# A later, shorter stretch for the second layer's weight conversion, with its first loads one pair ahead

## The chip, the cores and the metric

One core of a Trainium2 chip runs the whole kernel. The metric is device time in microseconds (us) of one execution; the kernel before was timed three times. The engines are named as the profile names them: PE (TensorE matmuls), PEld (its weight loads), DVE (VectorE), ACT (ScalarE), POOL (GpSimd) and SP (the queue that issues every DMA here). Each engine works through its own list of instructions strictly in the order in which it was written.

## The reference

Retention attention over 8 batches, 8 heads, 576 positions, then two feed-forward layers over the 4608 tokens:

```python
ret = scale * (q @ k.T) * Dmat          # Dmat[i, j] = gamma**(i - j), lower triangle
x = ret @ v                             # reshaped to 4608 x 512
h = x @ w_in;  x = (h - tanh(h)) @ w_out                    # first layer, d_ff = 2048
h = x @ w_in2; out = (h * sigmoid(1.702 * h)) @ w_out2      # second layer
```

The feed-forward weights arrive as float64, as pairs of 32-bit words.

## The kernel before

Tokens go in 9 tiles of 512 (`NTILE`), the hidden dimension in 8 pairs of two 128-wide columns. The main loop runs over 72 steps, one for each pair p of each tile t of layer 1; below, "pair (3,0)" is the first pair of the fourth tile. Every float32 operand is held as a high and a low float16 part and multiplied in three products. One step computes two `h` blocks on PE (`mm_in`, L534, 24 matmuls, two PSUM buffers `h`), the activation on ACT and DVE (`act1`), and, two steps behind (`LAG`), the second product into four `y` banks (`mm_out`, L650, 24 matmuls). `act1` on DVE is, for a pair, two `z` (L551, each of which ends the use of one `h` buffer), two passes over `w` (L554, L555), a predicated copy (L556) and `gl` (L558). When a tile is through, ACT evicts `y` (L657).

Into these steps other work is dealt out. `prep_steps` prepares the next tile: its input `yf` is loaded from DRAM into the one buffer that there is, its maximum taken (L446 on DVE, a reduction over partitions on POOL, L115), the scale `sx` worked out in small DVE instructions (L106 to L111), and the parts `xh` (ACT, L491) and `xl` (DVE, L496) written. `bg` holds the attention chunks that are left, five thirds of chunks a step. After `bg` the second layer's weights are converted by `conversion_steps(2, ...)`: 16 units of 1 MB each are loaded (`f`, two buffers), ACT takes magnitudes (L175), DVE clamps, shifts and joins the words (L180, L183, L190, L192) and finds a maximum per block; then each block is scaled, combined into seven sums for a Strassen-like product (`wsum`, L224 to L227) and split into `wsh` (ACT, L240) and `wsl` (DVE, L241), which SP writes to DRAM (`pd`, `od`). When the conversion is through, `load_pair` and `load_out` load these weights (`ws`, `woh`, `wol`; L672, L677) for layer 2 (PE L577, L625).

The program is recorded in the order of these loops, but a scheduler then orders each engine's instructions anew, with its own estimate of durations, before the kernel runs. So the order on the engines is not the order of the loops; it is fixed once the program is built. Attention, recorded by step 15, stands on PE up to pair (2,7). The pacing of the conversion is these lines of the main loop:

```python
elif conv2 is None:
    ...
    rate2 = len(conv2) / (n1 - LAST2 - i)
if conv2:
    todo_c += rate2
```

Of the kernel before, what the change touches and what calls it, by code (L numbers as in the profile page):

```python
# [47 lines left out]

LAG = 2
FIRST = 14  # L50
LAST2 = 10
NIP = 4
NF0 = 4
URGE = 600
# [20 lines left out]
def retention_two_ffn(ctx: ExitStack, tc: tile.TileContext, w1i, w1o, w2i, w2o, qt, kt, k, v, dq_d,  # L75
# [4 lines left out]
    def pool(name, bufs, space=None, to=ctx, side="left"):  # L80
        kw = {} if space is None else {"space": space}
        with tc.using_default_side(side):
            return to.enter_context(tc.tile_pool(name=name, bufs=bufs, reuse_waits="tile", **kw))
# [197 lines left out]
    def conversion_steps(l, kinds, w_in, w_out, fp, nf, wb, ahead, wp, also=None):  # L281
        units, load, magnitude, clamp, join, reduce, scale, split, bound, combine, split_seven = conversion(l, kinds, w_in, w_out, fp, wb, wp)
        blocks = [(kind, b) for kind in kinds for b in range(4)]
        steps = []

        def start():
            if also:
                also()
            for i in range(nf):
                load(i)  # L290
            magnitude(0)

        steps.append(start)
        for n, (kind, b) in enumerate(blocks):
            prev = blocks[n - 1] if n else None
            for u in range(2):
                i = 2 * n + u

                def one(i=i, u=u):
                    if not ahead and u == 0 and i:  # L300
                        magnitude(i)
                    clamp(i)
                    if ahead or u == 0:
                        magnitude(i + 1)

                def two(i=i):
                    join(i)
                    load(i + nf)

                steps += [one, two]  # L310
                if ahead and prev:
                    if u == 0:
                        steps.append(lambda p=prev: scale(*p))
                    steps.append(lambda p=prev, u=u: split(*p, u))
            steps.append(lambda kind=kind, b=b: reduce(kind, b))
            if (kind, b) == ("i", 3):
                steps.append(bound)
            if not ahead or n == len(blocks) - 1:
                steps.append(lambda kind=kind, b=b: scale(kind, b))
                if l == 2:  # L320
                    for q in range(2):
                        steps.append(lambda kind=kind, b=b, q=q: combine(kind, b, q))
                        steps.append(lambda kind=kind, b=b, q=q: split_seven(kind, b, q))
                else:
                    steps += [lambda kind=kind, b=b, u=u: split(kind, b, u) for u in range(2)]
        return deque(steps)
# [198 lines left out]
    def mm_in(l, t, c, hp_):  # L525
        o, j = L[l], jobs[l, t]
        blk, cc = divmod(c, 4)
        h = hp_.tile([P, TT], F32, tag="h", name="h")
        cs = slice(cc * P, (cc + 1) * P)
        n = 0  # L530
        for kd in range(KD):
            wh, wl = o.wih[blk][:, kd, cs], o.wil[blk][:, kd, cs]
            for w, x in ((wh, j.xh), (wh, j.xl), (wl, j.xh)):
                PE.matmul(h, w, x[:, kd, :], start=n == 0, stop=n == 3 * KD - 1)  # L534
                n += 1
        return h
# [4 lines left out]
    def act1(t, c, hs):  # L541

        j = jobs[1, t]
        blk = c // 4
        isig, sg = j.isig[:, blk : blk + 1], j.sg[:, 0:1]
        u, w, th, d, mk = wide("u"), wide("w"), wide("t"), wide("z"), wide("m", U8)
        gh, gl = wide("gh", F16, gp[-1]), wide("gl", BF16, gp[-1])
        for x, h in enumerate(hs):
            A.activation(out=u[:, x], in_=h, func=AF.Square, scale=isig)  # L549
            A.activation(out=th[:, x], in_=h, func=AF.Tanh, scale=isig)  # L550
            V.scalar_tensor_tensor(out=d[:, x], in0=h, scalar=isig, in1=th[:, x], op0=ALU.mult, op1=ALU.subtract)  # L551
        A.activation(out=w, in_=u, func=AF.Square, scale=SQ, bias=sqb)
        A.activation(out=mk, in_=th, func=AF.Square, scale=MASK_SCALE)
        V.scalar_tensor_tensor(out=w, in0=w, scalar=LEVEL, in1=u, op0=ALU.add, op1=ALU.mult)  # L554
        V.tensor_tensor(out=w, in0=w, in1=th, op=ALU.mult)  # L555
        V.copy_predicated(w, mk, d)  # L556
        A.activation(out=gh, in_=w, func=AF.Copy, scale=sg)  # L557
        V.scalar_tensor_tensor(out=gl, in0=w, scalar=sg, in1=gh, op0=ALU.mult, op1=ALU.subtract)  # L558
        newest[0] = d[:, 1, :1]
        for x in range(2):  # L560
            gtile[1, t, c + x] = gh[:, x], gl[:, x]
# [44 lines left out]
    def pair(t, p):  # L606
        act2(t, p, mm_pair(t, p))
# [61 lines left out]
    def load_pair(p):  # L669
        for parts, (sp, tag), src in zip((L[2].wih, L[2].wil), pair_slots(p), pair_d[p]):  # L670
            parts[p] = sp.tile([P, 7, 2, P], F16, tag=tag, name=f"ws{p}")
            SP.dma_start(parts[p], src)  # L672

    def load_out():
        for x, nm in enumerate(("woh", "wol")):
            w = wp2[0].tile([P, KF, DM], F16, tag=nm, name=nm + "2")
            SP.dma_start(w, out_d[x])  # L677
            setattr(L[2], nm, w)
# [9 lines left out]
    if True:  # L688
# [66 lines left out]
        conv2, cmb, loaded = None, [], False  # L755
        pre = deque()
        steps = [(t, p) for t in range(NTILE) for p in range(KF // 2)]
        n1 = len(steps)
        todo_c = 0.0
        for i in range(n1 + LAG):  # L760
            if i < n1:
                t, p = steps[i]
                act1(t, 2 * p, [mm_in(1, t, 2 * p + x, ps_h) for x in range(2)])
                if p == 1:
                    nl, nt = (1, t + 1) if t + 1 < NTILE else (2, 0)
                    items, scale_y = prep_steps(nl, nt)
                    pre.extend(items)
                    jobs[nl, nt].scale_y = scale_y
                for _ in range(2 if len(pre) > KF // 2 - p else 1):
                    if pre:  # L770
                        pre.popleft()()
                if bg:
                    for _ in range(min(5, len(bg))):
                        bg.popleft()()
                elif conv2 is None:
                    psa_scope.close()
                    att_scope.close()
                    ps_p.append(pool("ps_p", 2, PSUM))
                    fp = pool("fp2", 2, to=conv_scope, side="right")
                    wb = pool("wb2", 2, to=conv_scope, side="right")  # L780
                    cmb.append(pool("cmb", 1, to=conv_scope, side="right"))
                    stg = pool("stg", 2, to=conv_scope, side="right")
                    conv2 = conversion_steps(2, "io", w2i, w2o, fp, 2, wb, False, stg)
                    rate2 = len(conv2) / (n1 - LAST2 - i)
                if conv2:
                    todo_c += rate2
                    while conv2 and todo_c >= 1:
                        conv2.popleft()()
                        todo_c -= 1
                if conv2 is not None and not conv2 and not loaded:  # L790
                    loaded = True
                    conv_scope.close()
                    wp2.append(pool("wp2", 1))
                    for n in range(4):
                        load_pair(n)
                    load_out()
                    assert i < n1 - 8
                if t == NTILE - 1 and p in (5, 7):
                    load_pair(4 + p // 6)
            else:  # L800
                pair(0, i - n1)
            if i >= LAG:
                t, p = steps[i - LAG]
                for x in range(2):
                    mm_out(1, t, 2 * p + x)
# [58 lines left out]
```

## Time and profile before

| what | value |
|---|---|
| median of 3 runs | 1722.0 us (1721.31 to 1723.73) |
| the profiled execution | 1721.1 us |
| its span, first to last instruction | 1719.3 us |
| mean granted PE clock | 0.971 of full speed |
| PE busy | 1657.3 us, 96% |
| DVE busy | 1185.2 us, 69% |
| ACT busy | 847.3 us, 49% |

The profiled execution lies 0.9 us under the median; 1.8 us of it lie outside the span. Layer 1 runs from about 140 us to 1000 us, layer 2 from there to the end.

### The profile page before, as it was taken

What the parts mean: (1) busy time and instruction counts of PE and PEld (TensorE: products, weight loads), DVE (VectorE), ACT (ScalarE), POOL (GpSimd) and SP (SyncE); (2) the same over time, 40 slices, a digit from 0 to 9 for tenths busy, and PEclk for the clock granted to TensorE, in tenths of its full rate; (3) what the DMA queues carried; (4) which work ended last, traced back from release to release, by engine and by line L of the source; (5) the groups of instructions that cost most, each with busy time, mean ns of one, the idle gap of its engine ahead of it and who ended that gap; (6) DMA issues with size and microseconds to landing.
All of it is one profiled execution on the core that took longest, in us unless ns stands there. A gap on an engine that the chain in (4) does not pass through costs nothing.

```text
span 1719.3 us, 25499 instructions
## 1 busy us (share of the span) xinstructions
PE 1657.3 (96%) x10512; PEld 952.7 (55%) x10512; DVE 1185.2 (69%) x1982; ACT 847.3 (49%) x1263; POOL 31.5 (2%) x40
## 2 busy tenths in 40 slices
PE   5788999999979999999999999999999999999999
PEld 4664555555533444444444456666666666666665
DVE  7998665555589997998896864646556464646453
ACT  5556556556457676766666643333333232423222
POOL 0000000000000100000000000000000000000000
PEclk8668999999989999999999999999999999999999
DMA  9873324323053330432160120101011010100000
GB/s 336 277 247 118 107 86 120 99 74 115 22 196 113 116 106 11 123 104 76 37 236 25 68 93 1 50 1 50 1 50 44 7 50 1 50 1 25 1 25 25
DMA packets 111796, 141.36 MB, mean 82 GB/s; under 512 B 39488, under 2 KB 71360, under 8 KB 109248
## 3 DMA queue, kind: packets, MB, share of 16 engines
q1 hardware_dynamic: 111680, 139.73, 24.9%
q8 instruction: 82, 1.34, 0.3%
q14 instruction: 34, 0.28, 0.1%
HBM read 100.91 MB, written 38.80 MB: 81 GB/s over the span
## 4 chain that ended last, share of the span: by engine, by line
PE 88%; DVE 8%; DMA 2%; issue 1%; SPq 0%; ACT 0%; POOL 0%; POOLq 0%; ACTq 0%; DVEq 0%
PE yp L625 22%; PE y L650 21%; PE h L534 21%; PE pr L577 19%; PE pj L367 2%; PE op L384 2%; PE op L389 1%; DVE w L180 1%; DVE w L190 1%; PE up L406 1%; DVE w L192 1%; DVE pm L372 1%; DMA yf<-xd 1%; DVE wol L266 1%; DVE wil L266 1%
## 5 line engine op out<-in xcount | busy, mean ns | idle before, releaser
L577 PEld LDWEIGHTS <-ws 128*128 128x128 f16 x3024 | 295.9, 98 | 49.8
L534 PE MATMUL h<-xh,wih 128*128 128x512 f16 x576 | 222.6, 387 | 17.5 <-ACT xh L491 6.6
L534 PE MATMUL h<-xl,wih 128*128 128x512 f16 x576 | 222.2, 386 | 3.7 <-DVE xl L496 3.7
L534 PE MATMUL h<-xh,wil 128*128 128x512 f16 x576 | 222.1, 386 | 0.0
L650 PE MATMUL y<-gl,woh 128*128 128x512 bf16 x576 | 218.3, 379 | 0.4 <-DVE gl L558 0.4
L650 PE MATMUL y<-gh,wol 128*128 128x512 f16 x576 | 218.4, 379 | 0.0
L625 PE MATMUL yp<-woh,gh 128*128 128x512 f16 x576 | 218.3, 379 | 0.0
L625 PE MATMUL yp<-wol,gh 128*128 128x512 f16 x576 | 218.3, 379 | 0.0
L600 ACT ACTIVATE w<-u,isig 128x1024 f32<-128x1024 f32 x72 | 82.6, 1148 | 269.4 <-DVE u L598 269.4
L625 PE MATMUL yp<-woh,gl 128*128 128x512 f16 x576 | 214.9, 379 | 0.0
L577 PE MATMUL pr<-th,ws 128*128 128x256 f16 x1152 | 212.2, 273 | 0.0
L650 PE MATMUL y<-gh,woh 128*128 128x512 f16 x576 | 208.6, 379 | 0.7 <-ACT gh L557 0.7
L534 PEld LDWEIGHTS <-wih 128*128 128x128 f16 x1152 | 112.8, 99 | 155.9 <-issue 27.9
L650 PEld LDWEIGHTS <-woh 128*128 128x128 f16 x1152 | 112.1, 98 | 133.7 <-issue 1.3
L602 DVE SCALAR_TENSOR_TENSOR gl<-w,sg,gh 128x1024 f16<-128x1024 f32 x72 | 92.4, 1283 | 131.7 <-ACT gh L601 131.6
L625 PEld LDWEIGHTS <-gh 128*128 128x128 f16 x1152 | 112.7, 98 | 120.8
L549 ACT ACTIVATE u<-h,isig 128x512 f32<-128x512 f32 x144 | 98.4, 683 | 153.5 <-PE h L534 153.4
L577 PE MATMUL pr<-bh,ws 128*128 128x256 f16 x864 | 165.0, 273 | 0.0
L551 DVE SCALAR_TENSOR_TENSOR z<-h,isig,t 128x512 f32<-128x512 f32 x144 | 107.5, 747 | 81.9 <-ACT t L550 81.8
L577 PE MATMUL pr<-tl,ws 128*128 128x256 f16 x576 | 157.0, 273 | 0.0
L557 ACT ACTIVATE gh<-w,sg 128x1024 f16<-128x1024 f32 x72 | 82.6, 1147 | 94.2 <-DVE w L556 87.6
L558 DVE SCALAR_TENSOR_TENSOR gl<-w,sg,gh 128x1024 bf16<-128x1024 f32 x72 | 92.3, 1282 | 46.3 <-ACT gh L557 45.1
(112 smaller groups left out, 2312.8 us busy)
## 6 DMA issues: line engine op xcount, KB each, us to landing
f<-in_moe_w_in SPq DMA_DIRECT2D x16, 1024.0 KB, 7.4
f<-in_moe_w_out SPq DMA_DIRECT2D x16, 1024.0 KB, 6.2
yd<-ev SPq DMA_DIRECT2D x36, 256.0 KB, 2.8
yf<-yd SPq DMA_DIRECT2D x9, 1024.0 KB, 4.9
out<-z SPq DMA_DIRECT2D x36, 256.0 KB, 2.2
kT<-t_k SPq DMA_DIRECT2D x32, 256.0 KB, 2.9
qT<-t_q SPq DMA_DIRECT2D x32, 256.0 KB, 2.9
v<-n_v SPq DMA_DIRECT2D x32, 256.0 KB, 3.5
```

What stands on the lines that cost most here:

```text
L266: V.scalar_tensor_tensor(out=lo, in0=wv, scalar=s, in1=hi, op0=ALU.mult, op1=ALU.subtract)
L367: PE.matmul(o, a.kT[hs, hp, :T], a.qT[hs, hp, :T], start=True, stop=True)
L534: PE.matmul(h, w, x[:, kd, :], start=n == 0, stop=n == 3 * KD - 1)
L549: A.activation(out=u[:, x], in_=h, func=AF.Square, scale=isig)
L551: V.scalar_tensor_tensor(out=d[:, x], in0=h, scalar=isig, in1=th[:, x], op0=ALU.mult, op1=ALU.subtract)
L557: A.activation(out=gh, in_=w, func=AF.Copy, scale=sg)
L558: V.scalar_tensor_tensor(out=gl, in0=w, scalar=sg, in1=gh, op0=ALU.mult, op1=ALU.subtract)
L577: PE.matmul(ps, w, x[:, xi, k, :], start=i == 0, stop=i == 5)
L600: A.activation(out=g, in_=h, func=AF.Gelu_apprx_sigmoid, scale=isig)
L602: V.scalar_tensor_tensor(out=gl, in0=g, scalar=j.sg[:, 0:1], in1=gh, op0=ALU.mult, op1=ALU.subtract)
L625: PE.matmul(y, a[:, cs], b, start=p == 0 and x == 0 and r == 0, stop=last and x == 1 and r == 2)
L650: PE.matmul(ys[m], a, b, start=first and i == 0, stop=last and i == 2)
```

## The change

The conversion of the second layer's weights no longer begins in the step in which the attention queue is found empty (step 16, pair (2,0)), but in step 23, pair (2,7). In that step its pools are opened and its first item runs, which now only issues the loads of the first two units. The other 81 items are dealt out from step 24, pair (3,0), on, up to 6 steps ahead of the loop's end in place of 10: 81 items over 42 steps, where 82 items were dealt over 46. The first unit's magnitude, so far taken in the item that issues the loads, is taken in the item that clamps that unit. The instructions themselves are the same ones.

```diff
-LAST2 = 10
+LAST2 = 6
+CONV2 = 24
...
             for i in range(nf):
                 load(i)
-            magnitude(0)
+            if ahead:
+                magnitude(0)
...
-                    if not ahead and u == 0 and i:
+                    if not ahead and u == 0:
                         magnitude(i)
...
-                elif conv2 is None:
+                elif conv2 is None and i >= CONV2 - 1:
...
-                    rate2 = len(conv2) / (n1 - LAST2 - i)
-                if conv2:
+                    conv2.popleft()()
+                    rate2 = len(conv2) / (n1 - LAST2 - i - 1)
+                elif conv2:
                     todo_c += rate2
```

What the scheduler makes of it is seen in the built order. Line numbers of the changed kernel are one to three higher than those of the kernel before.

DVE at the end of pair (2,7), before. `w_3974` and `w_4500` are the first two blocks of the conversion, `f_...` their loaded units; `sx` and `xl_3` prepare tile 3.

```order
L109 TENSOR_SCALAR sx<-p_4315 128x1
L111 TENSOR_SCALAR sx<-p_4315 128x1
L109 TENSOR_SCALAR sg<-p_4587 128x1
L111 TENSOR_SCALAR sg<-p_4587 128x1
L511 TENSOR_SCALAR isig<-inv_in_110,sx 128x4
L516 TENSOR_SCALAR iy<-inv_out_112,sg 128x4
L180 TENSOR_SCALAR w_4500,mx_4501<-w_4500 128x4x256
L241 SCALAR_TENSOR_TENSOR wsl<-w_3974,s_in_115,wsh 128x256 x3
L183 TENSOR_SCALAR w_4500<-w_4500 128x4x256
L496 SCALAR_TENSOR_TENSOR xl_3_4321<-yf_3_4049,sx,xh_3_4320 128x1024
L190 SCALAR_TENSOR_TENSOR w_4500<-f_4059,w_4500 128x4x256
L496 SCALAR_TENSOR_TENSOR xl_3_4321<-yf_3_4049,sx,xh_3_4320 128x1024
```

Ahead of these rows, behind the two `z` of pair (2,7), stand the whole first block (two units and its four sums); behind them more of the second, and the first `z` of pair (3,0) is the 54th row after the last `z` of pair (2,7).

DVE in pair (1,7), changed kernel, where tile 3's `xl_3` now stands:

```order
L553 SCALAR_TENSOR_TENSOR z<-h,isig,t 128x512 x2
L498 SCALAR_TENSOR_TENSOR xl_3_4264<-yf_3_4021,sx,xh_3_4263 128x1024 x2
L556 SCALAR_TENSOR_TENSOR w<-w,u 128x1024
L557 TENSOR_TENSOR w<-w,t 128x1024
L558 COPY_PREDICATED w<-m,z 128x1024
L448 TENSOR_REDUCE mxx<-yf_4_4667 128x1 x2
L560 SCALAR_TENSOR_TENSOR gl<-w,sg,gh 128x1024
```

Tile 3's `xl` moved a whole tile ahead, and `sx` for it still further (to pair (1,0)). The conversion's first DVE rows now stand in pair (3,0), and no pair holds more than one block's work between its `z` and the next.

PE where the 24 `h` matmuls of pair (3,0) end, before; `h_4704` is the next pair's:

```order
L534 MATMUL h_4638<-xh1_3_4320,wih1_0_254 128x512
L534 LDWEIGHTS wih1_0_254
L534 MATMUL h_4638<-xl1_3_4321,wih1_0_254 128x512
L534 LDWEIGHTS wil1_0_255
L534 MATMUL h_4638<-xh1_3_4320,wil1_0_255 128x512
L534 LDWEIGHTS wih1_0_254
L534 MATMUL h_4704<-xh1_3_4320,wih1_0_254 128x512
```

The same place in the changed kernel, where 24 `y` matmuls of tile 2 follow:

```order
L536 MATMUL h_4554<-xh1_3_4263,wih1_0_254 128x512
L536 LDWEIGHTS wih1_0_254
L536 MATMUL h_4554<-xl1_3_4264,wih1_0_254 128x512
L536 LDWEIGHTS wil1_0_255
L536 MATMUL h_4554<-xh1_3_4263,wil1_0_255 128x512
L652 LDWEIGHTS woh1_1_831
L652 MATMUL y0_4108<-gh_4393,woh1_1_831 128x512
```

Before, 68 `y` matmuls stand together ahead of pair (3,0) and none behind it until the middle of pair (3,2); now 24 `h` and 24 `y` alternate there.

DVE in pair (3,7), before: ten rows from the pair's first `z` on, with the end of tile 5's preparation (`xl_5`).

```order
L551 SCALAR_TENSOR_TENSOR z<-h,isig,t 128x512
L224 TENSOR_TENSOR wsum<-w_5038 128x256
L225 TENSOR_TENSOR wsum<-w_5038 128x256
L551 SCALAR_TENSOR_TENSOR z<-h,isig,t 128x512
L496 SCALAR_TENSOR_TENSOR xl_5_5737<-yf_5_5462,sx,xh_5_5736 128x1024
L226 TENSOR_TENSOR wsum<-wsum,w_5038 128x256
L496 SCALAR_TENSOR_TENSOR xl_5_5737<-yf_5_5462,sx,xh_5_5736 128x1024
L558 SCALAR_TENSOR_TENSOR gl<-w,sg,gh 128x1024
L554 SCALAR_TENSOR_TENSOR w<-w,u 128x1024
L227 TENSOR_TENSOR wsum<-w_5038,wsum 128x256
```

The same pair in the changed kernel holds 27 rows from its first `z` to the next pair's; the last twelve are:

```order
L560 SCALAR_TENSOR_TENSOR gl<-w,sg,gh 128x1024
L513 TENSOR_SCALAR isig<-inv_in_110,sx 128x4
L556 SCALAR_TENSOR_TENSOR w<-w,u 128x1024
L242 SCALAR_TENSOR_TENSOR wsl<-w_5042,s_in_115,wsh 128x256
L557 TENSOR_TENSOR w<-w,t 128x1024
L242 SCALAR_TENSOR_TENSOR wsl<-w_5042,s_in_115,wsh 128x256 x2
L242 SCALAR_TENSOR_TENSOR wsl<-wsum,s_in_115,wsh 128x1024
L558 COPY_PREDICATED w<-m,z 128x1024
L242 SCALAR_TENSOR_TENSOR wsl<-w_5042,s_in_115,wsh 128x256 x3
L225 TENSOR_TENSOR wsum<-w_5042 128x256
L226 TENSOR_TENSOR wsum<-w_5042 128x256
L498 SCALAR_TENSOR_TENSOR xl_5_5665<-yf_5_5377,sx,xh_5_5664 128x1024 x2
```

Here a whole block's `wsl` and the preparation `xl_5` meet in one pair; pair (3,2) is like it, with `xl_4`. The other rows of pair (3,7) are two `z`, one copy L556 (in all two), two sums `wsum` (in all four) and 10 small ones (in all 11, up to L513). At the other end, the last `wsl` of the conversion stands in pair (7,7), and stood in pair (7,2).

## Rows read from the trace of the kernel before

**Rows 1.** The page: PE's busy time, and its granted clock in 40 slices.

```profile
PE 1657.3 (96%) x10512; PEld 952.7 (55%) x10512; DVE 1185.2 (69%) x1982; ACT 847.3 (49%) x1263; POOL 31.5 (2%) x40
...
PEclk8668999999989999999999999999999999999999
```

**Rows 2.** Waits of PE between 473 and 1000 us: total, times, longest.

```profile
PE h L534 <- ACT xh L491: 6.6, 1, 6.6
PE h L534 <- DVE m L200: 4.5, 1, 4.5
PE h L534 <- DVE z L551: 2.7, 1, 2.7
PE h L534 <- DVE xl L496: 1.0, 1, 1.0
PE y L650 <- ACT gh L557: 0.7, 1, 0.7
PE y L650 <- DVE gl L558: 0.4, 1, 0.4
```

**Rows 3.** Three stretches: length, busy PE, PEld, DVE, ACT, POOL (counts), clock, DMA share, GB/s.

```profile
477.10:491.80 14.70, 14.70 (x72) 6.67 (x69) 14.23 (x22) 6.99 (x9) 1.17 (x1) 1.00 0.29 89
491.80:556.53 64.73, 48.83 (x194) 20.26 (x193) 60.92 (x118) 43.76 (x59) 2.69 (x2) 0.87 0.47 165
556.53:603.15 46.62, 46.62 (x218) 21.14 (x216) 46.44 (x75) 31.38 (x42) 5.84 (x2) 1.00 0.30 107
```

**Rows 4.** The timeline of PE at the start of tile 3.

```profile
498.58 1.01 PE L534 MATMUL h<-xh,wih 128*128 128x512 f16 x2 [6.62 <-ACT xh L491]
...
501.41 0.63 PE L534 MATMUL h<-xh,wih 128*128 128x512 f16 x1
501.84 0.63 PE L534 MATMUL h<-xl,wih 128*128 128x512 f16 x1
```

**Rows 5.** The chain of work that ended last, pairs (3,5) and (4,1).

```profile
556.53 5.18 PE h L534 x24
...
597.97 5.18 PE h L534 x24
```

**Rows 6.** The timeline of DVE from the last `z` of tile 2 on.

```profile
476.69 0.75 DVE L551 SCALAR_TENSOR_TENSOR z<-h,isig,t 128x512 f32<-128x512 f32 x1 [1.84 <-ACT t L550]
...
492.78 0.14 DVE L106 TENSOR_SCALAR p<-arx 128x1 f32<-128x1 f32 x1
...
511.63 0.74 DVE L551 SCALAR_TENSOR_TENSOR z<-h,isig,t 128x512 f32<-128x512 f32 x1
...
617.97 0.74 DVE L551 SCALAR_TENSOR_TENSOR z<-h,isig,t 128x512 f32<-128x512 f32 x1
```

**Rows 7.** The timeline of ACT at 495 us.

```profile
495.09 1.21 ACT L175 ACTIVATE w<-f,zero 128x1024 f32<-128x1024 f32 x1 [2.41 <-DMA f<-in_moe_w_in]
```

**Rows 8.** DVE and ACT groups by form: count, busy us, mean ns.

```profile
L551 DVE SCALAR_TENSOR_TENSOR z<-h,isig,t 128x512 f32<-128x512 f32 x144 | 107.5, 747 | 81.9 <-ACT t L550 81.8
L496 DVE SCALAR_TENSOR_TENSOR xl<-yf,sx,xh 128x1024 f16<-128x1024 f32 x16 | 20.2, 1279 | 0.3 <-ACT xh L491 0.3
L241 DVE SCALAR_TENSOR_TENSOR wsl<-w,s_in,wsh 128x256 f16<-128x256 f32 x24 | 10.6, 477 | 0.0
L549 ACT ACTIVATE u<-h,isig 128x512 f32<-128x512 f32 x144 | 98.4, 683 | 153.5 <-PE h L534 153.4
```

**Rows 9.** The timeline of DVE at 600 us, where two instructions overlap.

```profile
600.10 1.21 DVE L554 SCALAR_TENSOR_TENSOR w<-w,u 128x1024 f32<-128x1024 f32 x1
601.24 1.28 DVE L558 SCALAR_TENSOR_TENSOR gl<-w,sg,gh 128x1024 bf16<-128x1024 f32 x1
```

**Rows 10.** The last load of layer 2's weights, its landing, and layer 2's first matmuls.

```profile
880.25 0.32 SPq L677 DMA_DIRECT2D wol<-od  x1
...
wol<-od SPq DMA_DIRECT2D x1, 2048.0 KB, 18.0
...
L577 PEld LDWEIGHTS <-ws x42: 98/98/98, 1001.6 to 1006.2; 128*128 128x128 f16 x42
```

More of the change, by code (lines that the diff above doesn't have):

```diff
@@ L796, in retention_two_ffn @@
                     load_out()
-                    assert i < n1 - 8
+                    assert i < n1 - 4
                 if t == NTILE - 1 and p in (5, 7):
```

## The prediction

> **What bounds the kernel now.** I read the page first. PE is busy for 96% of the span [rows 1], so every stretch in which PE has work sets the time; the only places to gain are those where PE is idle or slow. The granted clock shows two: the first slices, where the first layer's weights are converted (the change leaves the order there as it is), and a dent in slices 12 and 13, 473 to 559 us [rows 1]. The waits of PE from 473 to 1000 us [rows 2] all lie in that dent: 6.6 us on `xh`, 4.5, 2.7 and 1.0 us on DVE, 0.7 and 0.4 us on `gh` and `gl`, together 15.9 us. After 1000 us PE has none. So layer 1's remainder and all of layer 2 run at PE's pace, and what is won or lost in the dent goes through to the end one to one.
>
> How much is lost there? The idle time is not all of it. The chain shows 24 `h` matmuls in 5.18 us when PE is undisturbed [rows 5], 0.2158 us each. From the last `y` of tile 2 (491.8 us) to the start of pair (3,5) at 556.53 us the order holds five pairs' `h` (120) and 72 `y`, 192 matmuls (the window, which counts those that lap over its ends too, has 194 [rows 3]): 41.4 us of work in 64.7 us. **The loss is 23.3 us**: 15.9 us idle and 7.4 us slow. The slow part is the clock: behind the 6.62 us gap the matmuls follow at 0.43 us (501.41 to 501.84 [rows 4]), twice the undisturbed pitch, so the lower of its two levels, and the clock of the stretch is 0.87 [rows 3].
>
> By the Trainium skill (Perfetto Trace Analysis, Identifying the Most-Contended Engine) the busy share of matmuls is a poor measure and that of the weight loads a good one. The neighbouring windows have 0.454 us of weight loads per us; the 64.7 us could have held 29.4 us and held 20.3, so by that rule 9.1/0.454 = 20.0 us are lost, against 15.9 us by busy matmuls; the sum below would then end 3.3 us higher. I keep the count of matmuls.
>
> Why PE waits: DVE's timeline [rows 6] has the last `z` of tile 2 at 476.69 us, then almost nothing but conversion; the scale of tile 3 (`p<-arx`) comes only at 492.78 us, and the next `z` at 511.63 us, 34.9 us after the last. DVE is busy 14.2 of 14.7 us and then 60.9 of 64.7 us [rows 3]: its queue, in order, has the first block of the conversion ahead of tile 3's scale and half of the second ahead of pair (3,0)'s `z`. PE has no `xh`, then no free `h` buffer. ACT adds 2.4 us at 495.09 us, waiting for the third unit's load, with tile 3's `xh` and, by way of `wsh`, DVE behind it [rows 7].
>
> **The change, part by part.** *No instruction is added or removed*; PE's work is the same. All is in where things stand.
>
> *Tile 3's preparation.* `xl_3` now stands in pair (1,7) and `sx` earlier, so `xh` is there eight pairs before tile 3. That removes the 6.6 and 1.0 us, and the next tile's input no longer waits in SP's queue behind conversion writes. Cost: its reductions, 2 passes, and two `xl` go to pairs in which DVE has only activation and attention, well under a pair's 10.4 us.
>
> *The lump.* Between the `z` of (2,7) and of (3,0) stand only the activation and one mask, no conversion. PE's list has 24 `y` behind the 24 `h` of (3,0) where it had none for two and a half pairs, so a late `z` no longer stops it at once. This removes the 4.5 and 2.7 us, and with the gaps the slow clock. Gain so far: 23.3 us.
>
> *The conversion's own density.* 81 items over 42 pairs instead of 82 over 46 is 1.93 a pair instead of 1.78. What counts is the densest place. Instructions that follow each other overlap by about 0.08 us (600.10 to 601.24 is 1.14 us for a pass that shows 1.21 [rows 9]). So, from the durations of [rows 6, 8, 9] less 0.08, a `z` takes 0.67, a pass over `w` 1.14, `gl`, copy, `xl` and a full-width `wsl` 1.20, a narrow `wsl` 0.40, a sum (as wide) no more, a small one 0.06 us. Pair (3,7) is then 2 x 0.67 + 2 x 1.14 + 6 x 1.20 + 6 x 0.40 + 4 x 0.40 + 11 x 0.06 = 15.5 us of DVE against a pair's 48 x 0.2158 = 10.4 us of PE; pair (3,6), added up in the same way from its rows, 11.3. DVE falls 0.9 + 5.1 = 6.0 us behind by the `z` of (4,0). PE bears this as long as a `z` ends before the next pair's `h` needs its buffer, 10.4 us after its own `h` began. The earliest that it can end is 2.6 us of `h`, two ACT passes of 0.6 us net [rows 8], 0.75 us for itself and hand-overs, about 4.8: slack 5.6 us. The trace has the limit case: the `h` of (4,1) begins at 597.97 us [rows 5], so that of (4,2) at 608.3 and of (4,3) at 618.7; the `z` of (4,2) starts at 617.97 [rows 6], ends at 618.7, and PE waits for nothing. So (3,6) and (3,7) leak 0.4 us. Pairs (3,0) to (3,2) sum to 11.0, 8.5 and 15.5 us: 5.1 us behind at most, inside the slack, but a 1 MB `yf` load follows there and may add a microsecond. The bounds: nothing if the slack holds; if there were none, 6.0 + 5.1 us and 1.5 us of slow clock behind each gap (7.4 us over the five longer ones of [rows 2]), 14.1 us. The row of (4,2) lies near the slack's full length, so I take 1.3 us.
>
> *Loads one pair ahead.* Two units are loaded a pair before their magnitudes, which now stand behind pair (3,0)'s ACT work: the 2.4 us wait [rows 7] goes, with what it held up. It is inside the 23.3 us. If a load is late by as much again, ACT delays `gh` of (3,0), which PE needs two pairs later: nothing.
>
> *The end, five pairs later on DVE.* The last `wsl` moves from pair (7,2) to (7,7), 52 us. Behind it in SP's queue stand the loads for layer 2. Before, the last was issued at 880.25 us, lands 18.0 us later, at 898.3, and layer 2's first matmul is at about 1001.6 us [rows 10]: 103 us of cover, 51 us afterwards. Cost nothing; with the cover gone, a microsecond each.
>
> **Sum**, on the profiled execution: 1721.1 - 23.3 + 1.3 = 1699.1 us. The median lies 0.9 us above that execution: **1700.0 us**.
>
> **The rivals.** *A: DVE leaks.* The slack is smaller than I read, and pairs (3,2) and (3,7) each stop PE. For it: 15.5 us is half as much again as PE's own pair. Against it: the pairs behind them are light (5.7 us of DVE each), and the row of (4,2). Between 3 and 14.1 us of the gain go: about 1706 us. The Trainium skill (Perfetto Trace Analysis, Optimization Strategy) would have stretches with different busiest engines interleaved; the change leaves tile 2 without conversion and packs the rest, and by that rule A is likelier than I hold it.
>
> *B: the stall only moves.* The next tile's preparation meets the first block again, now at tile 4, and 23.3 us are lost there: 1722 us, no change. Against it: `xl_4` stands in pair (3,2), six pairs before it is needed.
>
> *C: slower.* Layer 2's weights come late. It decides from 51 us of further delay in the last `od` write on; DVE would have to fall five more pairs behind by tile 7. Each microsecond past that, and past the 22 us gained, adds to 1722; at 60 us more delay than planned with the gain lost, some 1731 us. Against it: the cover is three times as long as the load (18.0 us [rows 10]).
>
> **How the numbers follow.** The forecast, 1698 to 1703 us: 0.74. A: 0.18. B: 0.04. C: 0.02; the last 0.02 is a larger leak, up to 1718 us. The range 1696.8 to 1710 us holds the forecast and most of A; its lower end is the whole 23.3 us gained, and 2 us for a quieter start of tile 2 that I can't see. 0.2% of 1722 us, about what a measurement tells from no change, is 3.4 us. Faster: 0.74 + 0.18 + 0.02 = 0.94; same (B) 0.04; slower (C) 0.02.
>
> **What would show it.** Right: no clock dent near 500 us; PE waits in 400 to 1000 us of no more than 2 us together; `z` of (3,0) within 12 us of that of (2,7); layer 2's first matmul near 979 us. A: waits of `h` on `z` at about 515 to 520 and 560 us, longer than 1 us each. B: a wait on `xh` at tile 4. C: a wait of L577 on `ws` or L625 on `woh`. I am wrong if PE waits somewhere that is quiet now, above all in tiles 1 and 2, where DVE now holds tile 3's and 4's preparation between attention's masks.

## The result and the profile after

The changed kernel takes 1701.0 us (median of 4 runs, 1699.0 to 1702.7) against 1722.6 us for the kernel before (4 runs, 1721.3 to 1723.7): a ratio of 0.987, interval 0.9857 to 0.9884. The profiled execution took 1699.04 us, with a span of 1697.3 us.

The page first: PE's busy time, its granted clock in 40 slices, and the chain of work that ended last, by engine.

```profile
PE 1646.1 (97%) x10433; PEld 951.8 (56%) x10512; DVE 1184.2 (70%) x1982; ACT 846.2 (50%) x1263; POOL 34.5 (2%) x40
...
PEclk7668999999999999999999999999999999999999
...
PE 90%; DVE 6%; DMA 1%; issue 1%; SPq 0%; POOL 0%; ACT 0%; POOLq 0%
```

The dent [rows 1] is gone. (79 matmul records are missing in this trace, x10433 for 10512 weight loads, so PE's busy time reads a little low.) PE's waits from 473 to 1000 us were six groups with 15.9 us [rows 2]; now they are one line (total, times, longest):

```profile
PE h L536 <- DVE z L553: 0.3, 1, 0.3
```

Two long windows (length, busy PE, PEld, DVE, ACT, POOL, clock, DMA share, GB/s) show the full clock; what PE lacks of the length is the missing records and that 0.3 us.

```profile
172.00:473.00 301.00, 298.61 (x2209) 158.97 (x2241) 184.58 (x227) 169.61 (x324) 0.35 (x1) 1.00 0.31 92
473.00:1000.00 527.00, 524.25 (x2494) 243.81 (x2539) 471.64 (x706) 357.01 (x457) 22.53 (x17) 1.00 0.31 101
```

The chain, at the starts of pairs (3,1), (3,5) and (4,1), of which the last two answer to [rows 5]:

```profile
492.54 5.18 PE h L536 x24
...
533.98 5.20 PE h L536 x24
...
576.61 5.34 PE h L536 x24
```

Pair (3,5) starts at 533.98 us and no longer at 556.53: 22.55 us earlier; the gain lies ahead of this pair. Pair (4,1) shows where the one wait lies. DVE's timeline has the first `z` of pairs (3,6), (3,7) and (4,0) (start, duration):

```profile
549.20 0.75 DVE L553 SCALAR_TENSOR_TENSOR z<-h,isig,t 128x512 f32<-128x512 f32 x1
...
560.59 0.74 DVE L553 SCALAR_TENSOR_TENSOR z<-h,isig,t 128x512 f32<-128x512 f32 x1
...
575.83 0.73 DVE L553 SCALAR_TENSOR_TENSOR z<-h,isig,t 128x512 f32<-128x512 f32 x1
```

and on PE the `h` of (4,1) waits for the last of these:

```profile
576.61 0.38 PE L536 MATMUL h<-xh,wih 128*128 128x512 f16 x1 [0.33 <-DVE z L553]
```

**A measure without the scatter.** The runs of one kernel lie up to 10 us apart, and the variants below differ by 4. So I look where the scatter sits. Each pair has 24 weight loads for `h`; the 193rd is therefore the first of pair (1,0). It is a mark behind which PE is nearly always busy. Timelines of PE's weight loads at this mark, before:

```profile
244.23 0.10 PEld L534 LDWEIGHTS <-wih 128*128 128x128 f16 x1
```

the changed kernel:

```profile
244.82 0.10 PEld L536 LDWEIGHTS <-wih 128*128 128x128 f16 x1
```

and the changed kernel run once more (after_again, below), with a span of 1699.5 us:

```profile
247.01 0.10 PEld L536 LDWEIGHTS <-wih 128*128 128x128 f16 x1
```

From the mark to the end of the span (behind the mark, from here on) the two profiles of the changed kernel take 1697.3 - 244.8 = 1452.5 us and 1699.5 - 247.0 = 1452.5 us; the kernel before takes 1719.3 - 244.2 = 1475.1 us. **Behind the mark the change gives 22.6 us.** What differs from run to run lies ahead of it: the mark came between 243.9 and 251.6 us in the twelve profiles of this study.

### The profile page after: what moved, and what is told of

It reads as the page before. It is cut to its first block, busy times and chain, and to the rows that moved or that the text cites. A ratio compares the mean times of both kernels' runs of the same rounds, so it can differ in the third digit from the quotient of the medians.

```text
span 1697.3 us, 25426 instructions
## 1 busy us (share of the span) xinstructions
PE 1646.1 (97%) x10433; PEld 951.8 (56%) x10512; DVE 1184.2 (70%) x1982; ACT 846.2 (50%) x1263; POOL 34.5 (2%) x40
## 4 chain that ended last, share of the span: by engine, by line
PE 90%; DVE 6%; DMA 1%; issue 1%; SPq 0%; POOL 0%; ACT 0%; POOLq 0%
PE yp L627 22%; PE h L536 21%; PE y L652 21%; PE pr L579 19%; PE pj L369 3%; PE op L386 2%; PE op L391 2%; DVE w L191 1%; PE up L408 1%; DVE w L181 1%; DVE w L193 1%; DVE pm L374 0%; DMA xd<-xe 0%; DMA f<-in_moe_w_in 0%; DVE qT L357 0%
## 5 line engine op out<-in xcount | busy, mean ns | idle before, releaser
L579 PEld LDWEIGHTS <-ws 128*128 128x128 f16 x3024 | 295.9, 98 | 49.8
L627 PE MATMUL yp<-woh,gh 128*128 128x512 f16 x576 | 218.3, 379 | 0.0
L627 PE MATMUL yp<-wol,gh 128*128 128x512 f16 x576 | 218.3, 379 | 0.0
L627 PE MATMUL yp<-woh,gl 128*128 128x512 f16 x576 | 214.9, 379 | 0.0
L652 PE MATMUL y<-gh,woh 128*128 128x512 f16 x576 | 212.8, 379 | 0.0
L579 PE MATMUL pr<-th,ws 128*128 128x256 f16 x1152 | 212.2, 273 | 0.0
L652 PE MATMUL y<-gl,woh 128*128 128x512 bf16 x497 | 188.4, 379 | 0.0
L627 PEld LDWEIGHTS <-gh 128*128 128x128 f16 x1152 | 112.7, 98 | 120.8
L579 PE MATMUL pr<-bh,ws 128*128 128x256 f16 x864 | 165.0, 273 | 0.0
L579 PE MATMUL pr<-tl,ws 128*128 128x256 f16 x576 | 157.0, 273 | 0.0
L579 PE MATMUL pr<-bl,ws 128*128 128x256 f16 x432 | 117.8, 273 | 0.0
```

The lines of the kernel that those rows point to most:

```text
L579: PE.matmul(ps, w, x[:, xi, k, :], start=i == 0, stop=i == 5)
L627: PE.matmul(y, a[:, cs], b, start=p == 0 and x == 0 and r == 0, stop=last and x == 1 and r == 2)
L652: PE.matmul(ys[m], a, b, start=first and i == 0, stop=last and i == 2)
```

## The experiments

Each run's time behind the mark is read as above, against the 1452.5 us of the changed kernel; "idle" is the sum of PE's waits from 473 to 1000 us. Diffs are against the changed kernel unless something else is said.

| run | median us | ratio to before | behind the mark | idle |
|---|---|---|---|---|
| before | 1722.6 | | +22.6 | 15.9 |
| after_again | 1700.8 | 0.9856 to 0.9913 | 0.0 | 0.3 |
| place_only | 1702.7 | 0.9867 to 0.9899 | +0.9 | 0.9 |
| late_no_split | 1705.6 | 0.9876 to 0.9923 | +4.0 | 4.1 |
| end0 | 1704.5 | 0.9872 to 0.9916 | +4.2 | 3.9 |
| conv23 | 1705.3 | 0.9878 to 0.9920 | +4.4 | 2.9 |
| nosplit23 | 1704.3 | 0.9868 to 0.9924 | +4.4 | 3.0 |
| dense18 | 1707.8 | 0.9891 to 0.9932 | +6.1 | 5.6 |
| pace_only | 1716.1 | 0.9940 to 0.9974 | +12.9 | 11.0 |
| split_only | 1716.3 | 0.9938 to 0.9968 | +15.1 | 11.5 |
| dense26 | 1726.7 | 1.0010 to 1.0031 | +27.1 | 17.5 |

### The parts alone

Below, the *gate* is the step in which the conversion is opened (`CONV2`), the *early loads* are the item that only issues loads, and the *rate* goes by the end of the conversion (`LAST2`). **late_no_split** takes back the early loads; **split_only** has nothing but them (with `CONV2 = 1` the gate opens in step 16, as before); **pace_only** is the kernel before with the thinner rate alone; **place_only** has the new gate and the early loads, with the old end.

```diff
 late_no_split
-            if ahead:
-                magnitude(0)
+            magnitude(0)
...
-                    if not ahead and u == 0:
+                    if not ahead and u == 0 and i:
 split_only
-LAST2 = 6
-CONV2 = 24
+LAST2 = 10
+CONV2 = 1
 pace_only, against before
-LAST2 = 10
+LAST2 = 6
...
-                    assert i < n1 - 8
+                    assert i < n1 - 4
 place_only
-LAST2 = 6
+LAST2 = 10
```

> The changed kernel with the first magnitude put back into the item that issues the loads; start (step 23) and end (6 steps ahead) stay. If the place of the conversion does it (tile 3's preparation ahead of it, no block between the z of (2,7) and (3,0)): 1699 to 1702 us, since in its built order DVE, added up pair by pair against 10.36 us of PE, falls at most 5.0 us behind. If the loads one pair ahead do it (the 2.4 us wait of ACT with tile 3's xh behind it): several us slower than the changed kernel, 1704 us or more, and ACT waits for f on the first unit.

> The split of loads and magnitude alone: the conversion is opened as before when the attention queue is empty (step 16) and ends as before (10 steps ahead). In its built order xl_3 stands in pair (1,7) as in the changed kernel, but pair (3,3) holds 18.3 us of DVE and DVE falls up to 14.7 us behind at (3,4). By the place, with a slack of 5.6 us: no wait on xh, about 9 us idle in waits of h on z, and some 4 us of slow clock, 1712 us (1707 to 1716). If the loads ahead do it: 1699 to 1702 us. If tile 3's preparation alone did the harm: about 1700 us too, as xl_3 is early here.

> The kernel before with LAST2 = 6 alone (82 items over 50 pairs; magnitude with the loads). Its built order also has xl_3 in pair (1,7), a lump of 18.3 us in pair (3,3), and DVE up to 14.7 us behind at (4,0). By lateness beyond the slack: like split_only, 1712 us (1707 to 1716). If the density of items is what counts (1.64 a pair, the lowest of all): as fast as the changed kernel or faster.

> The new gate and the early loads, but the conversion still ends where it did before (LAST2 = 10): 33 pairs of conversion in place of 37. The order of the first dozen pairs after the gate is that of the changed kernel, so by the theory of lateness the whole gain is there: from the first h of pair (1,0) to the first L579 matmul 735 to 738 us (changed kernel 734.8, kernel before 757.4), 1700 to 1704 us, TensorE waiting less than 3 us between 400 and 1000. Rival (the thinning carries a good part of the gain, as the run with the pace alone had 6.5 us of it): 742 us or more between these two marks, 1707 to 1712 us.

place_only keeps all but 0.9 us of the 22.6 (735.7 us from the mark to the first weight load of L579, 734.8 in the changed kernel): the gate, with the early loads, is the gain. It differs from split_only in `CONV2` alone, and so **the gate by itself is worth 15.1 - 0.9 = 14.2 us**, although its items are dealt out more densely (81 over 38 steps, against 81 over 45). The early loads alone give 22.6 - 15.1 = 7.5 us, the rate alone 9.7 us. These don't add up with the rest, for each of the four runs has `xl_3` in pair (1,7) of its order, as the changed kernel has, and in none does PE wait on `xh` or `xl` any more. What split_only and pace_only still lose stands for the most part in tile 3, where the lump now is. Both took slightly longer than the 1707 to 1716 us expected: 11.0 to 11.5 us of waits in place of 9, of which the theory had counted those on `z` only. PE's waits from 473 to 1000 us in split_only:

```profile
PE h L536 <- DVE z L553: 5.3, 3, 2.8
PE y L652 <- DVE gl L560: 3.7, 1, 3.7
PE y L652 <- ACT gh L559: 2.5, 1, 2.5
```

So removing the wait on `xh` is not enough; the piled-up conversion stops PE a few pairs later, by other rows. SP's timeline shows that the gate does not work by a later first load. That load, in split_only

```profile
479.18 0.39 SPq L153 DMA_DIRECT2D f<-in_moe_w_in  x1
```

and in the changed kernel

```profile
479.23 0.38 SPq L153 DMA_DIRECT2D f<-in_moe_w_in  x1
```

stands 234.4 us behind the mark in both (marks at 244.76 and 244.82 us), and SP waits there for the last of attention's masks on DVE (`pm`, which ends at 479.20 us in the changed kernel). What the gate changes is how many items of the conversion already stand in the program ahead of tile 3's steps when that point comes. By the code, the gate of before opens at step 16, and items come out of it for seven pairs that can't run before that point; with `CONV2 = 24` only the first loads do. The traces show the pile. DVE's clamps (L181, one for each unit of 1 MB) from the first `z` of pair (3,0) to that of (3,4), in split_only (486.06 to 542.79 us)

```profile
L181 DVE TENSOR_SCALAR_CACHE_REDUCE w<-w 128x1024 f32<-128x1024 f32 x4 | 4.9, 1218 | 1.0 <-ACT w L176 1.0
```

and in place_only (490.25 to 535.06 us):

```profile
L181 DVE TENSOR_SCALAR_CACHE_REDUCE w<-w 128x1024 f32<-128x1024 f32 x2 | 2.4, 1210 | 0.0
```

All the conversion's rows on DVE (L175 to L242) sum to 32 us there in split_only and to 17 us in place_only, for the same four pairs of PE; the stretch takes 56.7 and 44.8 us.

late_no_split loses 4.0 us, and its 1705.6 us lie where the early loads were to count, but not in the way that the prediction gave them: ACT waits for no `f` there at all, as in the changed kernel. PE's waits:

```profile
PE y L651 <- DVE gl L559: 2.3, 1, 2.3
PE y L651 <- ACT gh L558: 1.0, 1, 1.0
PE h L535 <- DVE z L552: 0.8, 1, 0.8
```

DVE's timeline ahead of the longest of them: a sum's `wsl` and two maximum passes of the next tile stand ahead of a `gl`.

```profile
581.73 1.26 DVE L242 SCALAR_TENSOR_TENSOR wsl<-wsum,s_in,wsh 128x1024 f16<-128x1024 f32 x1
582.92 2.33 DVE L447 TENSOR_REDUCE mxx<-yf 128x1 f32<-128x1024 f32 x2
585.18 1.21 DVE L556 TENSOR_TENSOR w<-w,t 128x1024 f32<-128x1024 f32 x1
586.31 1.27 DVE L559 SCALAR_TENSOR_TENSOR gl<-w,sg,gh 128x1024 bf16<-128x1024 f32 x1
```

The changed kernel has its two maximum passes at the same place, at 581.28 us, but there the `gl` of this pair (3,7) stands ahead of them, and PE reads it 3.0 us after its end:

```profile
577.48 1.26 DVE L560 SCALAR_TENSOR_TENSOR gl<-w,sg,gh 128x1024 bf16<-128x1024 f32 x1
...
581.79 0.38 PE L652 MATMUL y<-gl,woh 128*128 128x512 bf16 x1
```

So I had the 4 us down to the order that is built, and tried that next.

### The gate one pair earlier, with and without the early loads

**conv23** and **nosplit23**:

```diff
 both
-CONV2 = 24
+CONV2 = 23
 nosplit23 also
-            if ahead:
-                magnitude(0)
+            magnitude(0)
...
-                    if not ahead and u == 0:
+                    if not ahead and u == 0 and i:
```

> The new conversion with its gate one pair earlier (CONV2 = 23). The gate is not what holds its first VectorE work, which stands in pair (3,0) as before, but the rate falls a little and the rows of the order fall otherwise: no pair in which VectorE owes more than 4 us by the durations of the trace. Theory of lateness: no wait at all of TensorE on VectorE between 400 and 1000 us, 1698 to 1701 us, not distinguishable from the changed kernel (0.3 us of wait there). Rival (the gate's own place counts, since the fourth tile's beginning is the busy place): a wait on h or xh of 2 us or more in tile 3 and 1704 to 1722 us.

> As the run with CONV2 = 23, but with the block's first magnitude put back into the step that issues the loads. VectorE's total in each pair differs by 0.1 us at most from the run with the split. If the split acts only through the order that is built (theory after the first four runs): equal to the run with the split within 1 us, 1698 to 1702 us, although ScalarE may wait for f at L176 by some us. If the split is worth its 4 us by itself, by ScalarE's wait on the load: 1703 to 1706 us.

Behind the mark the two agree (1701.1 - 244.2 and 1708.5 - 251.6, both 1456.9 us), and ACT waits for no `f` in nosplit23 either: **with the gate this late, the early loads by themselves are worth nothing measurable**, and their 4.0 us in late_no_split came from the order that they happened to change. But conv23 did not come out as expected, and neither did the time of nosplit23: 4.4 us slower than the changed kernel. No `z` is late, as I had worked out; a `gl` is. DVE's timeline in conv23:

```profile
525.75 1.28 DVE L242 SCALAR_TENSOR_TENSOR wsl<-wsum,s_in,wsh 128x1024 f16<-128x1024 f32 x1
526.94 2.35 DVE L448 TENSOR_REDUCE mxx<-yf 128x1 f32<-128x1024 f32 x2
529.19 1.23 DVE L557 TENSOR_TENSOR w<-w,t 128x1024 f32<-128x1024 f32 x1
530.33 1.29 DVE L560 SCALAR_TENSOR_TENSOR gl<-w,sg,gh 128x1024 bf16<-128x1024 f32 x1
```

and PE's, which goes on as soon as that `gl` is written (530.33 + 1.29 = 531.62):

```profile
531.67 0.38 PE L652 MATMUL y<-gl,woh 128*128 128x512 bf16 x1 [2.65 <-DVE gl L560]
```

The same four rows, in nearly the same order, stand ahead of the wait of late_no_split. The sum closes with the clock of the 10 us in which the wait lies, 0.83:

```profile
530.00:540.00 10.00, 8.33 (x31) 3.45 (x31) 10.00 (x14) 5.23 (x5) 0.00 (x0) 0.83 0.01 3
```

2.65 us, 0.3 us on an eviction and 0.17 x 10 = 1.7 us of clock, less the 0.3 us that the changed kernel waits too, are 4.3 us, against 4.4 measured. So my theory after the first four runs held (the split acts through the order alone), and the tally behind it, which looked at `z` only, did not: `gl` is a second deadline.

### The dose: a denser conversion

**dense18** and **dense26** end the conversion twelve and twenty pairs earlier.

```diff
 dense18
-LAST2 = 6
+LAST2 = 18
 dense26
-LAST2 = 6
+LAST2 = 26
```

> The new conversion ended twelve pairs earlier (LAST2 = 18), between the changed kernel (6) and the one with 26. By the trace's durations VectorE is late by up to 8.9 us at a z, against a slack of 5.6 us. Theory of lateness: it leaks 8.9 - 5.6 = 3.3 us at that place and little elsewhere, with some slow clock after a wait of that size: 1702 to 1707 us, TensorE waiting 3 to 5 us between 400 and 1000 us. Rival (the loss grows evenly with the density of the conversion: 25.7 us for 20 pairs fewer, so 12/20 of it): 1716 us.

> The changed kernel with LAST2 = 26: 81 items over 22 pairs, 3.7 a pair. Start and split as in the changed kernel. In its order DVE is up to 22.8 us behind in tiles 4 and 5, never more than 10 us added in one pair. With a slack of 5.6 us: 17 us idle, spread over waits of h on z from (4,0) to (5,3), and 0 to 8 us of slow clock: 1716 to 1724 us. If the density of the conversion does not matter as long as the start is late: 1699 to 1703 us.

PE's waits from 473 to 1000 us in dense18

```profile
PE h L536 <- DVE z L553: 2.4, 2, 1.5
PE h L536 <- DVE m L209: 1.6, 1, 1.6
PE y L652 <- DVE gl L560: 1.4, 1, 1.4
PE y L652 <- ACT gh L559: 0.2, 1, 0.2
```

and in dense26

```profile
PE h L536 <- DVE z L553: 10.7, 3, 5.2
PE y L652 <- DVE gl L560: 3.2, 1, 3.2
PE y L652 <- ACT ev L659: 2.1, 3, 1.7
PE y L652 <- ACT gh L559: 1.5, 2, 0.8
```

The loss grows faster than the density: +0.9 us for four pairs fewer (place_only), 6.1 for twelve, 27.1 for twenty. That is what a slack does, and speaks against a loss in proportion. The size was a little off for dense18 (1707.8 us, 1702 to 1707 expected): 5.6 us of waits where 3.3 us and "little elsewhere" were expected, 1.4 of them again on `gl`. The 1.6 us that the view puts down to `m`, which `h` does not read, are a wait on a `z` as well: PE goes on when that `z` is written (592.28 + 0.74 = 593.02), with `m` right behind it.

```profile
592.28 0.74 DVE L553 SCALAR_TENSOR_TENSOR z<-h,isig,t 128x512 f32<-128x512 f32 x1
...
593.08 0.38 PE L536 MATMUL h<-xh,wih 128*128 128x512 f16 x1 [1.59 <-DVE m L209]
```

So is the 4.5 us of [rows 2], where a `z` ends at 512.37 us and PE goes on at 512.43. dense26 is slower than the kernel before, and than the 1716 to 1724 us expected: its waits are longer than those of [rows 2] (17.5 against 15.9 us), and 27.1 + 0.3 - 17.5 = 9.9 us more go beside the waits, as slower clock: its windows of 40 us from 520 to 760 us have 0.91, 0.96, 0.99, 0.93, 1.00 and 0.96. The expected waits (17 us) were right, the slow clock (0 to 8 us) too small.

### The late end

**end0** lets the conversion run to the last pair that the program allows.

```diff
-LAST2 = 6
+LAST2 = 0
...
-                    assert i < n1 - 4
+                    assert i < n1
```

> The new conversion, but spread to the last pair that the schedule allows (LAST2 = 0): its last step falls in pair (8,4) and no longer in (7,7), five pairs or 5 x 10.36 = 52 us later. In the changed kernel 57.6 us lay between the last weights' landing and the first L579 matmul. Theory of lateness (the prediction's): only what DVE owes at a deadline costs time; here it is late by more than 4 us in one pair only, so layer 1 leaks about nothing, and the cover is still some 5 us: 1698 to 1702 us, the last landing 2 to 10 us ahead of its first matmul. Rival (C of the prediction): the weights come late for layer 2, TensorE waits at its start and falls to the slow clock: 1705 to 1715 us, with a wait of the second layer's matmuls on a DMA or on the weights' transposes.

The last two loads on SP, in the changed kernel

```profile
903.81 0.55 SPq L679 DMA_DIRECT2D woh<-od  x1
904.97 0.32 SPq L679 DMA_DIRECT2D wol<-od  x1
```

and in end0:

```profile
967.81 0.32 SPq L679 DMA_DIRECT2D woh<-od  x1
968.95 0.32 SPq L679 DMA_DIRECT2D wol<-od  x1
```

64 us later, and PE waits for neither `ws`, `woh` nor `wol`. The 4.2 us (1704.5 us, 1698 to 1702 expected) are for the most part again a `gl` behind `wsl` and `mxx`, now in tile 4 (2.3 us), a `z` at 962 us (1.2) and another at 953 us (0.4). My expectation named the wrong first use: `wol` is not read by L579 but by L627, which starts in end0 at

```profile
1004.40 0.38 PE L627 MATMUL yp<-woh,gh 128*128 128x512 f16 x1
```

The load lands 17.1 us after its issue, at 986.1 us, so it has 18.3 us of cover left. The load with the least cover is another one, the first `ws` of layer 2's first pair, which L579's first weight load needs:

```profile
962.08 0.42 SPq L674 DMA_DIRECT2D ws<-pd  x1
...
968.24 0.53 PEld L579 LDWEIGHTS <-ws 128*128 128x128 f16 x4
```

It lands 5.7 us after its issue, at 967.8 us: 0.4 us of cover. In this order four matmuls of L579 stand at 968.45 us, 10 us ahead of the others, so end0 is about as late as its own order bears.

### The changed kernel again

**after_again** is the changed kernel without an edit.

> The changed kernel once more, on the chip of the run beside it. If the scatter of the times is all in the first 172 us, where TensorE waits and its clock is below full speed, then between the first h of pair (1,0) and the first L579 matmul it takes 734.8 us again, to 0.3 us, and the time follows the first mark alone (244.8 us in the first profile): 1697 to 1706 us. If layer 1 scatters too, the 734.8 comes out by a microsecond or more different, and the 4 us between the changed kernel and its neighbours may be scatter.

The mark came 2.2 us later than in the first profile; from it to the first weight load of L579 (981.8 us) it took 734.8 us again, and to the end 1452.5 us again. The 4 us between the changed kernel and its neighbours are no scatter. The 2.2 us between its two profiles lie ahead of the mark; where the 8 us between its other runs lie (1700.3 to 1708.4 here), which have no profile, is not shown.

## Why the prediction was right

*The loss of 23.3 us, counted in matmuls.* The dent was read off as slices 12 and 13; the row of the clock shows it in slice 12 alone, and the trace before has 0.84 in slice 12 and 0.96 in slice 13. The loss itself was worked out from the order: 22.6 us came back behind the mark, with 0.3 us of wait left. The count of matmuls was the right measure of it. By the rule on weight loads that the prediction weighed (the Trainium skill, Perfetto Trace Analysis, Identifying the Most-Contended Engine) 20.0 us would have been lost, which is less than came back; the weight loads, too, run longer at the lower clock (in the kernel before, 11 took 1.57 us at a granted clock of 0.50 from 500 to 505 us, and 24 took 2.27 us at full clock from 600 to 605 us), so their busy time hides a part of such a loss.

*The preparation and the lump.* The prediction gave the two together all of the gain: 7.6 us of the waits to the early preparation, 7.2 us to the lump. The mechanism stands (the first `z` of (3,0) came at 486.11 us, 9.7 us after the last of (2,7), in place of 34.9), but the weights differ: the early preparation of tile 3 alone, which split_only and pace_only have, left 12.9 to 15.1 us of the loss in place, as 11.0 to 11.5 us of waits on `z`, `gl` and `gh` and as slower clock. It is not the gate's doing either: pace_only, with the old gate, has it too, and why the order of the kernel before lacks it no run tells. The gate is what breaks up the lump (place_only against split_only). Rival B, that the stall only moves, is what these two runs show in part: it moved from `xh` in tile 3's first pair to rows a few pairs on.

*The density.* Pair (3,7) was worked out at 15.5 us of DVE, (3,6) at 11.3. From the first `z` of (3,7) to the first of (4,0) the trace has 575.83 - 560.59 = 15.24 us, and 560.59 - 549.20 = 11.39 us for (3,6). The light pairs were mis-sized: 5.7 us of DVE each were worked out, and from the first `z` of (4,0) to that of (4,1), and likewise in (3,3), the trace has 7.71 us without a gap. The difference is the two maximum passes (`mxx`), 2.33 us there; 5.7 comes out if they are priced as small instructions. These are the rows behind which the `gl` of four variants was late. The leak at (4,1) was to be 0.4 us and is 0.33. The microsecond that I added for the `yf` load behind (3,2) did not come: PE waits for nothing there. So the term of 1.3 us was 1.0 us too large. The profiled execution took 1699.04 us, 1699.1 forecast, although its mark came 0.6 us later than that of the profile before. The median of 1701.0 us against 1700.0 is off by less than the scatter ahead of the mark. That the slack ends where I had it was the right guess for `z` only; `y` on `gl` has a deadline of its own, which I had no term for, and the changed kernel's order happens to keep it, by 3.0 us at the place where late_no_split misses it. That was luck. Had it not, some 4 us would have gone, as in four of the variants, in which 2.3 to 2.7 us of them were the wait on `gl`: rival A by another row than I named. By the rule of interleaving stretches (the Trainium skill, Perfetto Trace Analysis, Optimization Strategy) A was likelier than I held it; the packed conversion cost 0.3 us of wait at this density, and 6.1 us more at that of dense18.

*Loads one pair ahead.* "Inside the 23.3 us" was right in that there is no separate term, but the reason was not shown: the ACT wait of 2.4 us [rows 7] is also gone without the early loads, once the gate is late (late_no_split, nosplit23), and with the early loads and the old gate (split_only) ACT waits 4.0 us for `f`.

*The end.* Layer 2's first L579 matmul came at 979.8 us, 979 expected. The cover was undercounted: `wol`, issued at 904.97 us, landed 17.0 us later, and L627, which reads it, starts at 1001.2 us: 79 us of cover and not 51. The load that L579 does read, `ws` of the first pair, landed at 903.8 us, 76 us ahead of its first use. A delay of 64 us more (end0) met every first use without a wait, by 0.4 us, so rival C's point of decision, 51 us, was set too early by at least 13 us.

## What to carry to other kernels

When work for a spare engine is dealt out ahead of the point at which it can run, it piles up there as a lump; open the gate where it can start, and the same work at nearly the same rate hides. To see whether it hides, add up the spare engine's queue from one deadline to the next, for every row that the busy engine waits for (here `z`, `gl` and `gh`, not `z` alone): lateness under the slack cost nothing here, and beyond it a wait counted one to one, with a slower clock on top for some of the waits. Where runs scatter, find a mark behind which they agree, and compare from there.

## What the runs showed that I had not expected

Two executions of the same program agree to 0.1 us from the mark to the end (1452.5 us), while the stretch ahead of it takes anything from 243.9 to 251.6 us. Waits of nearly the same length had different prices: 2.65 us in conv23 came with a clock of 0.83 over 10 us (1.7 us more), while late_no_split, with 2.28 us, kept the full clock in the 10 us in which its wait ended:

```profile
587.00:597.00 10.00, 9.37 (x44) 4.29 (x44) 8.62 (x9) 6.87 (x9) 0.00 (x0) 1.00 0.29 107
```

What sets the difference these runs do not tell.
